# Seven block products on 320 and 256 columns in place of 384 and 192, and a re-searched order of work

## The chip, the cores and the metric

The kernel runs on one core of one Trainium2 chip. Its time is device microseconds from one execution of the whole program; a figure for a kernel is the median of several executions. The core's engines work side by side, each through its own instructions in order, and wait for one another through semaphores: PE (TensorE, the matrix products), DVE (VectorE), ACT (ScalarE), POOL (GpSimd) and SP (SyncE, which only issues transfers here). PE writes to PSUM, eight banks of 512 float32 columns; all else lies in SBUF.

## The reference, cut to what matters

```
a      = softmax of phi over 32 memory slots, per head and token
k_m, v_m = a.T @ k, a.T @ v                     # 32 x 64 per head
attn   = softmax(q @ k_m.T / 8) @ v_m           # 4 x 576 tokens, 8 heads of 64
x      = attn, as 2304 tokens x 512
h      = x @ w_in;  x = (h * sigmoid(1.702 h)) @ w_out          # d_ff 2048
xn     = x / sqrt(mean(x * x) + 1e-6) * rms_g
g      = xn @ w_gate;  val = xn @ w_val                         # d_ff 1536
out    = (g * sigmoid(g) * val) @ w_out2                        # 2304 x 512
```

All in float32. The weights are read as 64-bit numbers and converted on the chip.

## The kernel before, in words

**Tiling.** The four batches of 576 tokens are two pairs of 1152 tokens, `pr` 0 and 1. Activations stand transposed: channels on partitions, tokens along the columns. Float32 products are made of float32r halves: an operand x is held as h (a rounded copy) and l = x - h, and a product is h·h + l·h + h·l. `split` (L745) makes such a pair: a copy on ACT, a subtraction on DVE or POOL. Every matmul has weights of 128x128 that are loaded for it alone, so the instructions on PE are LDWEIGHTS, MATMUL, LDWEIGHTS, MATMUL and so on.

**Stages.** First the attention of the first pair, with the loading and converting of weights; then the first MLP in steps `a_g1` and `a_g2` for `pr` 0 (8 groups of 256 hidden channels), beside it the attention of the second pair; the same for `pr` 1, beside it the norm of the first pair (`norm_1` to `norm_4`); then the second MLP of the first pair (`b_g3`, `b_g4`, 6 groups), beside it the norm of the second pair and the block sums `t_a` to `t_d`; last the second MLP of the second pair, `s_g3` and `s_g4`.

**The last stage.** The second pair's gate and value products are done as a two-by-two block product with seven products in place of eight. The blocks of the activations are 256 channels by 576 tokens (`tba` to `tbd`), those of the weights 256 channels by 128 outputs, and there are 12 groups `f`. `product(q, a, b, f)` (L1321) makes one block product on one of two column ranges `q`, `WIDE[q]` (L1318), columns 0 to 384 and 384 to 576: 6 matmuls into one PSUM bank (two halves of the channels by three terms). Here a product on the first range is called wide, on the second narrow. `s_g3(f, k)` (L1335) calls it for both ranges of all seven: for `k` 0 three block products, for 1 two, for 2 two. Their results are added up on DVE by `plus` (L1332) in four sums `part[q]`; two get a Silu on ACT; each is multiplied with its partner, and the two products of 576 columns, end to end 1152 tokens, are split into three tiles of 384 tokens. The list `to` (L1370) says which columns of which range go to which tile: five splits for each `f`. `s_g4(g, kk)` (L1382) multiplies 128 tokens of two `f` with the output weights, 6 matmuls of 512 columns, and adds into `oacc` on DVE; after the last group `put` writes them out.

**The order.** Nothing of this is issued where it is called. Each operation goes into a list (`Plan.add`, L268), and `Plan.order` (L438) then plays the list through on a model of the engines, with the durations of `Plan.cost` (L307), the buffers of each pool and PSUM, and a due time for each step (`dues`, L397). The operation that can start first goes first, among near ones that with the earliest due time. What comes out is one fixed order for each engine. For a float32r matmul of n columns the model has 0.0135 + n/2400 us (L316). Where PE has nothing to do in the model for long, `fill` (L521) puts in matmuls of 512 columns on constants. Two tables bend this: `HASTE` (L127) makes a named step's due time earlier by so many us, and `OTHER` (L171) moves the named operations of a step (counted from 0 within the step) from POOL to DVE or from DVE to POOL.

Of the kernel before, what the change touches and what calls it, by code (L numbers as in the profile page):

```python
# [10 lines left out]
F32 = mybir.dt.float32  # L11
# [20 lines left out]
class Fill:  # L32
    eng, name = "PE", "matmul"
# [83 lines left out]
class Plan:  # L117
# [18 lines left out]
        "a_g2 0 4 0": 38.2,  # L136
        "a_g2 0 6 0": 22.8,
        "a_g2 0 7 0": 33.4,
        "a_g2 1 1 0": 38.0,
        "a_g2 1 6 2": 45.6,  # L140
        "a_g2 1 7 2": 18.7,
        "att_k3 2 1": 46.5,
# [6 lines left out]
        "att_q3s 0 0 1": 69.7,  # L149
        "att_q4 1 1 0": 86.2,  # L150
        "att_q4 3 0 1": 21.3,
        "b_g4 0 2": 6.4,
        "ld_unit 2 1": 51.8,
        "norm_1 0 1": 60.9,
        "norm_1 1 0": 22.4,
        "norm_2 0 2": 20.2,
        "norm_3 0 1": 66.6,
        "norm_4 0 0 0": 9.7,
        "norm_4 0 0 1": -36.4,
        "s_g3 0 2": 27.8,  # L160
        "s_g4 5 1": 73.1,
        "s_g4 5 5": 13.4,
        "s_g4 5 7": 18.7,
        "s_g4 5 8": 62.3,
        "vm_part 0 3 0": 31.7,
        "vm_part 0 7 0": 56.5,
        "w_conv a 0 2 in 0": 50.3,
        "w_load a 0 7 in 0": 87.4,
    }

    OTHER = {  # L171
        "a_g1 0 0 0": (17,),
        "a_g1 0 0 1": (17,),
        "a_g1 0 1 0": (8, 17),
        "a_g1 0 1 2": (8,),
        "a_g1 0 2 2": (8, 10),
# [13 lines left out]
        "a_g1 0 6 2": (8, 19),  # L190
        "a_g1 0 6 3": (17,),
        "a_g1 0 7 0": (17,),
        "a_g1 0 7 1": (8, 10, 19),
        "a_g1 1 2 0": (17,),
        "a_g1 1 2 1": (21,),
        "a_g1 1 2 2": (8,),
        "a_g1 1 3 0": (8, 17),
        "a_g1 1 4 2": (10, 21),
        "a_g1 1 5 2": (21,),
        "att_k3 1 0": (2,),  # L200
        "att_k3 2 1": (2,),
        "att_q3s 0 0 1": (3,),
        "att_q3s 0 1 0": (3,),
        "att_q3s 1 0 0": (3,),
        "att_q3s 2 0 0": (3,),
        "att_q3s 2 1 1": (3,),
        "att_q3s 3 0 0": (3,),
        "att_q3s 3 0 1": (3,),
        "norm_1 0 0": (3,),
        "norm_1 0 1": (3,),  # L210
        "norm_1 0 2": (2, 5),
        "norm_4 0 0 2": (2,),
        "norm_4 0 0 3": (2,),
        "s_g3 11 2": (39,),
        "t_b 0 0": (1,),
        "w_conv a 0 0 in 1": (1,),
        "w_conv a 0 1 in 1": (1, 7),
        "w_conv a 0 1 out 0": (7,),
        "w_conv a 0 1 out 1": (1, 7),
        "w_conv a 0 2 in 0": (1,),  # L220
        "w_conv a 0 2 out 0": (1,),
        "w_conv a 0 3 in 0": (7,),
        "w_conv a 0 3 in 1": (7,),
        "w_conv a 0 3 out 0": (1,),
# [11 lines left out]
        "w_conv a 0 7 out 1": (1,),  # L236
        "w_conv a 1 0 in 0": (1,),
        "w_conv a 1 0 in 1": (1,),
        "w_conv a 1 0 out 0": (1,),
        "w_conv a 1 1 out 1": (1,),  # L240
        "w_conv a 1 5 in 0": (1,),
        "w_conv a 1 5 in 1": (1,),
        "w_conv a 1 6 in 0": (1,),
        "w_conv a 1 6 in 1": (1,),
        "w_conv a 1 6 out 0": (1,),
        "w_conv a 1 6 out 1": (1,),
    }

    def __init__(self, nc):
# [56 lines left out]
    @staticmethod  # L306
    def cost(op):  # L307
        def size(x):
            return reduce(int.__mul__, (n for s, n in x.ap[1:]), 1)

        n = size(op.out)
        if op.eng == "PE":
            if op.name == "transpose":
                return 0.0009 * n, 0.0009 * n + 0.16
            if op.kw["lhsT"].dtype == F32R:
                t = 0.0135 + n / 2400  # L316
                return t, t + 0.16
            t = 0.094 if size(op.kw["lhsT"]) == 32 else 0.17 if n > 1 else 0.22
            return t, t + 0.25
        if op.eng == "ACT":  # L320
            t = 0.08 + n / 1200
            if op.ins[0].space == bass.MemoryType.PSUM:
                t += 0.13 if op.kw.get("func") is AF.Gelu_apprx_sigmoid else 0.07
            return t, max(t + 0.04, 0.18 + n / 1200)
        if op.eng == "POOL":
            two = op.name == "tensor_tensor"
            each = 0.00215 if two else 0.00104 if op.kw.get("op0") is ALU.mult else 0.00355
            if op.kw.get("op") is ALU.mult:
                each = 0.0016
            t = 0.05 + each * n + (0.1 if two else 0.0)  # L330
            return t, t + 0.05
        if op.eng == "DVE":
            rate = 1920 if Plan.fast(op) else 960
            if op.name == "tensor_reduce":
                n, rate = size(op.ins[0]), 960 if op.ins[0].ap[-1][0] == 1 else 560
            t = 0.075 + n / rate + (0.04 if n < 20 else 0.0)
            if any(x.space == bass.MemoryType.PSUM for x in op.ins):
                t += 0.04
            return t, t + 0.08
        return 0.47, 0.0  # L340
# [213 lines left out]
def kernel(  # L554
# [24 lines left out]
    nc = tc.nc  # L579
    B, H, S, D = q.shape  # L580
    M = phi.shape[3]
# [4 lines left out]
    P = 128  # L586
# [8 lines left out]
    TB = 384  # L595
# [9 lines left out]
    def pool(name, bufs, space=bass.MemoryType.SB, **kw):  # L605
        return Slots(plan, ctx.enter_context(tc.tile_pool(name=name, bufs=bufs, space=space)), bufs, **kw)
# [3 lines left out]
    cvp = pool("cv", 6, spare=3)  # L610
# [22 lines left out]
    def psum(name):  # L633
        return psp.tile([P, 512], F32, tag="ps", name=name)
# [110 lines left out]
    def split(x, h, l, eng=V):  # L745
        A.copy(out=h, in_=x)
        sub_lo(eng, l, x, h)
# [567 lines left out]

    WIDE = (slice(0, TB), slice(TB, S))  # L1318
    part = {}

    def product(q, a, b, f):  # L1321
        ps, n = psum("ps_" + a), WIDE[q]
        ps = ps[:, : n.stop - n.start]
        a, b = wt["s", f][a], tb[b]
        i = 0
        for y, z in ((0, 0), (1, 0), (0, 1)):
            for e in range(2):
                PE.matmul(ps, lhsT=a[y][:, e], rhs=b[:, z, e, n], start=(i == 0), stop=(i == 5))
                i += 1
        return ps  # L1330

    def plus(q, to, x, y):  # L1332
        V.tensor_tensor(out=part[q][to], in0=part[q][x], in1=y, op=ALU.add)

    def s_g3(f, k):  # L1335
        if k == 0:
            part[0] = [cvp.tile([P, 512], F32, tag="cv", name="c")[:, :TB] for i in range(4)]
            c = [vlp.tile([P, 512], F32, tag="vl" + x, name="c") for x in "hl"]
            part[1] = [x[:, o : o + S - TB] for x in c for o in (0, S - TB)]
            for q in range(2):  # L1340
                A.copy(out=part[q][0], in_=product(q, "A11", "B11", f))
            for q in range(2):
                plus(q, 1, 0, product(q, "S2", "T2", f))
            for q in range(2):
                plus(q, 0, 0, product(q, "A12", "B21", f))
        elif k == 1:
            for q in range(2):
                plus(q, 2, 1, product(q, "S3", "T3", f))
            for q in range(2):
                part[q].append(product(q, "S1", "T1", f))  # L1350
                plus(q, 1, 1, part[q][4])
        else:
            for q in range(2):
                plus(q, 3, 2, product(q, "A22", "T4", f))
                A.activation(out=part[q][3], in_=part[q][3], func=AF.Silu)
                plus(q, 2, 2, part[q][4])
                A.activation(out=part[q][2], in_=part[q][2], func=AF.Silu)
            for q in range(2):
                plus(q, 1, 1, product(q, "S4", "B22", f))
            if f % 3 < 2:  # L1360
                ts = [gpp.tile([P, 2, TB], F32R, tag="gp", name="pp") for i in range(NTB)]
            else:
                x = tb["tbd"][:, 1].rearrange("p y e n -> p (y e n)")
                ts = [
                    x[:, 2 * TB * i : 2 * TB * (i + 1)].rearrange("p (y n) -> p y n", y=2)
                    for i in range(NTB)
                ]
            pt["s", f] = ts
            H = TB // 2
            to = [  # L1370
                [(0, 0, 0, TB)], [(1, 0, 0, H)],
                [(1, H, 0, H), (2, 0, H, TB)], [(2, H, 0, H)],
            ]
            for q in range(2):
                for j, (x, y) in enumerate(((0, 3), (1, 2))):
                    o = part[q][x]
                    V.tensor_tensor(out=o, in0=o, in1=part[q][y], op=ALU.mult)
                    for i, d, c0, c1 in to[2 * j + q]:
                        d = slice(d, d + c1 - c0)
                        split(o[:, c0:c1], ts[i][:, 0, d], ts[i][:, 1, d])  # L1380
# [112 lines left out]
    for j, (*key, t) in enumerate(slots):  # L1493
        i = groups.index(tuple(key))
# [39 lines left out]
    for j, (*key, t) in enumerate(slots):  # L1534
        key = tuple(key)
        i = groups.index(key)
# [93 lines left out]
```

## Time and profile before

| | |
|---|---|
| median of 3 runs | 869.61 us (869.45 to 871.04) |
| the profiled execution | 867.26 us, its span 865.5 us |
| granted TensorE clock, mean of the span | 1.000 |
| busy: PE, PEld (weight loads) | 853.2 us (99%), 813.3 us (94%) |
| busy: DVE, ACT, POOL | 668.8 us (77%), 459.3 us (53%), 285.3 us (33%) |

The span is the time from the first to the last instruction of the profiled execution. A busy time is the time covered by an engine's instructions. Successive matmuls overlap in the records, so the duration of one is longer than the time by which it delays the next; the distance between starts is what it takes of PE.

### The profile page before, as it was taken

The numbers are of one execution on the slowest core, as the hardware profiler recorded it, in microseconds if no ns is written. First come the engines' busy times: TensorE is split into PE (matmuls) and PEld (weight loads), VectorE is DVE, ScalarE is ACT, GpSimd is POOL, SyncE is SP. The second block draws the span as 40 slices with busy tenths as digits, with TensorE's granted clock in tenths as the row PEclk, the third lists the DMA queues.
The fourth block names the chain that finished last, engine by engine and source line by source line (L and its number), as shares of the span: only waits on it lengthen the run. The fifth ranks groups of instructions, "written<-read, shape, count | busy, mean of one in ns | idle before, by whom it ended". The sixth has DMA issues, their size and how long they took to land.

```text
span 865.5 us, 15423 instructions
## 1 busy us (share of the span) xinstructions
PE 853.2 (99%) x5644; PEld 813.3 (94%) x5644; DVE 668.8 (77%) x1409; ACT 459.3 (53%) x1073; POOL 285.3 (33%) x308
## 2 busy tenths in 40 slices
PE   8899999999999999999999999999999999999998
PEld 6799999999999999999999999999999999999996
DVE  3979899999962774577786778586679878989875
ACT  3587777767668654564555645333244543433320
POOL 2354565363488675555443233221000000000000
PEclk9999999999999999999999999999999999999999
DMA  9975549734612111242462525331132111202003
GB/s 244 273 209 145 172 122 276 216 83 132 155 51 61 37 49 50 62 146 68 152 218 75 169 99 171 110 121 51 36 104 82 48 38 38 62 13 62 13 1 109
DMA packets 60508, 93.54 MB, mean 108 GB/s; under 512 B 5392, under 2 KB 29968, under 8 KB 60432
## 3 DMA queue, kind: packets, MB, share of 16 engines
q1 hardware_dynamic: 60432, 92.56, 37.0%
q8 instruction: 44, 0.72, 0.4%
q14 instruction: 32, 0.26, 0.1%
HBM read 69.99 MB, written 22.54 MB: 107 GB/s over the span
## 4 chain that ended last, share of the span: by engine, by line
PE 89%; DVE 5%; issue 2%; DMA 2%; ACT 1%; SPq 1%; POOL 0%; DVEq 0%; ACTq 0%; POOLq 0%
PE pg L550 66%; PE ps_S L550 10%; PE ps_A L550 7%; PE pvm L550 2%; PE pq L550 2%; DMA raw_a_out<-in_moe_w_out_dram 2%; DVE pad L550 1%; DVE stage L550 1%; PE pk L550 1%; DVE x L550 1%; SPq L550 1%; DVE kmisc L550 0%; PE pnm L550 0%; ACT pad L550 0%; ACT vm_6h L550 0%
## 5 line engine op out<-in xcount | busy, mean ns | idle before, releaser
L550 PE MATMUL pg<-gr,a_outh 128*128 128x384 f32 (+1 forms) x736 | 196.6, 334 | 0.5 <-POOL gr L550 0.5
L550 PEld LDWEIGHTS pg<-gr,a_outh 128*128 128x128 f32 x736 | 132.9, 188 | 1.6 <-POOL gr L550 1.0
L550 DVE TENSOR_TENSOR x<-x,pg 128x384 f32<-128x384 f32 (+1 forms) x172 | 90.4, 539 | 46.2 <-PE pg L550 44.9
L550 PE MATMUL pg<-gr,a_outl 128*128 128x384 f32 (+1 forms) x368 | 122.0, 331 | 0.0
L550 POOL TENSOR_TENSOR gr<-gf,gr 128x288 fp32r<-128x288 f32 (+2 forms) x135 | 86.5, 660 | 75.2 <-ACT gr L550 49.8
L550 POOL TENSOR_TENSOR tbd<-c,tbd 128x192 fp32r<-128x192 f32 x1 | 0.6, 604 | 250.9 <-ACT tbd L550 250.9
L550 DVE TENSOR_TENSOR oacc<-oacc,pg 128x512 f32<-128x512 f32 x90 | 61.6, 685 | 25.1 <-PE pg L550 23.9
L550 PE MATMUL pg<-b_o2h,pp 128*128 128x512 f32 x216 | 70.7, 393 | 0.0
L550 ACT ACTIVATE gf<-pg 128x288 f32<-128x288 f32 x128 | 51.1, 411 | 35.4 <-PE pg L550 30.2
L550 PEld LDWEIGHTS pg<-gr,a_outl 128*128 128x128 f32 x368 | 69.1, 188 | 0.0
L550 ACT CAST gr<-gf 128x288 fp32r<-128x288 f32 (+2 forms) x184 | 59.3, 360 | 9.8 <-PE pg L550 5.4
L550 DVE TENSOR_TENSOR c<-c,ps_S 128x384 f32<-128x384 f32 (+1 forms) x120 | 53.5, 452 | 14.0 <-PE ps_S L550 10.8
L550 PE MATMUL pg<-s_o,pp 128*128 128x512 f32 x216 | 57.0, 393 | 0.0
L550 DVE TENSOR_TENSOR pf<-sg,pg 128x384 f32<-128x384 f32 x36 | 19.9, 552 | 37.5 <-PE pg L550 25.3
L550 PEld LDWEIGHTS pg<-b_o2h,pp 128*128 128x128 f32 x216 | 40.6, 188 | 8.0
L550 PE MATMUL ps_S<-tbc,s_S 128*128 128x192 f32 (+1 forms) x288 | 47.3, 305 | 0.0
L550 PE MATMUL ps_S<-tbb,s_S 128*128 128x192 f32 (+1 forms) x288 | 47.1, 305 | 0.0
L550 PE MATMUL ps_A<-tba,s_A 128*128 128x192 f32 (+1 forms) x288 | 46.9, 305 | 0.0
L550 PEld LDWEIGHTS pg<-s_o,pp 128*128 128x128 f32 x216 | 39.7, 188 | 7.5
L550 PEld LDWEIGHTS ps_S<-tbc,s_S 128*128 128x128 f32 x288 | 43.9, 190 | 1.1
L550 PEld LDWEIGHTS ps_A<-tba,s_A 128*128 128x128 f32 x288 | 43.4, 190 | 0.7
L550 PEld LDWEIGHTS ps_S<-tbb,s_S 128*128 128x128 f32 x288 | 43.2, 190 | 0.6
(248 smaller groups left out, 2156.8 us busy)
## 6 DMA issues: line engine op xcount, KB each, us to landing
cache<-cv SPq DMA_DIRECT2D x36, 256.0 KB, 2.8
raw_a_in<-in_moe_w_in_dram SPq DMA_DIRECT2D x16, 512.0 KB, 5.3
raw_a_out<-in_moe_w_out_dram SPq DMA_DIRECT2D x16, 512.0 KB, 4.2
cache<-pad SPq DMA_DIRECT2D x32, 256.0 KB, 5.1
raw_b_gate<-in_moe_w_gate_dram SPq DMA_DIRECT2D x12, 512.0 KB, 4.6
raw_b_val<-in_moe_w_val_dram SPq DMA_DIRECT2D x12, 512.0 KB, 4.5
raw_b_o<-in_moe_w_out_dram SPq DMA_DIRECT2D x12, 512.0 KB, 4.1
raw_s_vg<-cache SPq DMA_DIRECT2D x48, 128.0 KB, 2.7
```

The source lines that it names most:

```text
L550: getattr(self.real[op.eng], op.name)(*op.args, **op.kw)
```

## The change

The two column ranges of a block product become 0 to 320 and 320 to 576. The four sums of each range get these widths, and the list `to` is written anew, as the tile borders at 384 and 768 now fall elsewhere: six splits for each `f`, one of them of 64 columns. The planner's duration of a float32r matmul gets a lower bound of 0.109 us. In `HASTE` 11 entries are gone, in `OTHER` entries for 27 operations; no entry is added. As most of these steps name POOL in the code and `OTHER` had them on DVE, 22 operations go from DVE to POOL: nine `sub_lo` of `a_g1` (four of 288 columns, two of 192, three of 96), eight of `w_conv` for `pr` 1 (512 columns), two additions of 384 columns and one of 768 in `norm_1` and its `sub_lo` of 384, and one multiplication in `att_q3s`. Five go from POOL to DVE: one `tensor_scalar` in `w_conv a 0 2 out 0`, two `sub_lo` in `norm_4`, one subtraction in `t_b`, one `sub_lo` in `s_g3 11 2`.

```diff
 HASTE
-        "a_g2 1 1 0": 38.0,
-        "b_g4 0 2": 6.4,
-        "norm_1 0 1": 60.9,
-        "norm_1 1 0": 22.4,
-        "norm_3 0 1": 66.6,
-        "norm_4 0 0 0": 9.7,
-        "norm_4 0 0 1": -36.4,
-        "s_g3 0 2": 27.8,
-        "s_g4 5 1": 73.1,
-        "s_g4 5 7": 18.7,
-        "w_conv a 0 2 in 0": 50.3,
 OTHER
-        "a_g1 0 0 1": (17,),
-        "a_g1 0 7 1": (8, 10, 19),
-        "a_g1 1 2 0": (17,),
-        "a_g1 1 2 1": (21,),
-        "a_g1 1 2 2": (8,),
-        "a_g1 1 3 0": (8, 17),
-        "a_g1 1 4 2": (10, 21),
-        "a_g1 1 5 2": (21,),
+        "a_g1 0 7 1": (10, 19),
+        "a_g1 1 4 2": (21,),
-        "att_q3s 1 0 0": (3,),
-        "norm_1 0 0": (3,),
-        "norm_1 0 1": (3,),
-        "norm_1 0 2": (2, 5),
-        "norm_4 0 0 2": (2,),
-        "norm_4 0 0 3": (2,),
-        "s_g3 11 2": (39,),
-        "t_b 0 0": (1,),
-        "w_conv a 0 2 out 0": (1,),
-        "w_conv a 1 0 out 0": (1,),
-        "w_conv a 1 1 out 1": (1,),
-        "w_conv a 1 5 in 0": (1,),
-        "w_conv a 1 5 in 1": (1,),
-        "w_conv a 1 6 in 0": (1,),
-        "w_conv a 1 6 in 1": (1,),
-        "w_conv a 1 6 out 0": (1,),
-        "w_conv a 1 6 out 1": (1,),
 cost
-                t = 0.0135 + n / 2400
+                t = max(0.0135 + n / 2400, 0.109)
...
-    WIDE = (slice(0, TB), slice(TB, S))
+    WIDE = (slice(0, 320), slice(320, S))
...
-            part[0] = [cvp.tile([P, 512], F32, tag="cv", name="c")[:, :TB] for i in range(4)]
+            part[0] = [cvp.tile([P, 512], F32, tag="cv", name="c")[:, :320] for i in range(4)]
             c = [vlp.tile([P, 512], F32, tag="vl" + x, name="c") for x in "hl"]
-            part[1] = [x[:, o : o + S - TB] for x in c for o in (0, S - TB)]
+            part[1] = [x[:, o : o + 256] for x in c for o in (0, 256)]
...
-            H = TB // 2
             to = [
-                [(0, 0, 0, TB)], [(1, 0, 0, H)],
-                [(1, H, 0, H), (2, 0, H, TB)], [(2, H, 0, H)],
+                [(0, 0, 0, 320)], [(0, 320, 0, 64), (1, 0, 64, 256)],
+                [(1, 192, 0, 192), (2, 0, 192, 320)], [(2, 128, 0, 256)],
             ]
```

## Rows read from the trace of the kernel before

**Rows 1.** Windows over the whole span; columns named in the first line.
```profile
core 0: us, PE busy (x) PEld busy (x) DVE busy (x) ACT busy (x) POOL busy (x), PEclk, DMA share, GB/s
0.00:60.00 60.00, 53.77 (x519) 45.52 (x520) 39.94 (x112) 33.51 (x86) 21.69 (x27) 1.00 0.96 255
60.00:240.00 180.00, 178.15 (x1435) 174.06 (x1434) 171.60 (x366) 135.53 (x339) 94.34 (x92) 1.00 0.56 159
240.00:637.70 397.70, 397.70 (x2344) 384.94 (x2343) 270.37 (x509) 208.55 (x456) 168.69 (x190) 1.00 0.31 96
637.70:861.30 223.60, 223.56 (x1352) 208.79 (x1351) 186.19 (x424) 81.75 (x196) 0.60 (x1) 1.00 0.17 49
```

**Rows 2.** Chain that ended last, in order of time: start us, us, what.
```profile
252.11 3.21 PE pg L550 x24
298.23 1.43 PE pvm L550 x12
641.57 0.65 PE ps_A L550 x6
642.22 1.40 PE pg L550 x6
643.62 1.07 PE ps_A L550 x6
644.69 1.04 PE ps_S L550 x6
645.73 2.76 PE pg L550 x12
650.60 1.32 PE ps_S L550 x12
654.30 1.72 PE ps_A L550 x12
```

**Rows 3.** Groups by form, PE then DVE and ACT, 637.7 to 861.3 us.
```profile
L550 PE MATMUL ps_A<-tba,s_A 128*128 128x192 f32 x144 | 19.5, 271 | 0.0
...
L550 DVE TENSOR_TENSOR pp<-c,pp 128x192 fp32r<-128x192 f32 x32 | 10.4, 352 | 1.0 <-ACT pp L550 0.9
L550 DVE TENSOR_TENSOR pp<-c,pp 128x384 fp32r<-128x384 f32 x8 | 4.4, 552 | 0.1
...
L550 ACT CAST pp<-c 128x192 fp32r<-128x192 f32 x32 | 10.0, 352 | 13.9 <-DVE c L550 13.8
L550 ACT CAST pp<-c 128x384 fp32r<-128x384 f32 x8 | 4.1, 509 | 1.0 <-DVE c L550 0.7
```

**Rows 4.** Timeline of DVE near the end: start us, us, instruction [idle before].
```profile
854.28 0.36 DVE L550 TENSOR_TENSOR tbd<-c,tbd 128x192 fp32r<-128x192 f32 x1 [0.47 <-ACT tbd L550]
861.30 0.69 DVE L550 TENSOR_TENSOR oacc<-oacc,pg 128x512 f32<-128x512 f32 x1 [0.67 <-PE pg L550]
```

**Rows 5.** Groups by form on POOL, whole span.
```profile
L550 POOL TENSOR_TENSOR gr<-gf,gr 128x288 fp32r<-128x288 f32 x51 | 43.8, 866 | 44.5 <-ACT gr L550 29.7 <-PE pg L550 11.3 <-issue 3.2
L550 POOL TENSOR_SCALAR pad<-pad 128x512 f32<-128x512 f32 x14 | 29.9, 2138 | 15.2 <-ACT pad L550 15.2
L550 POOL TENSOR_TENSOR a_outl<-raw_a_out,a_outh 128x512 fp32r<-128x512 f32 x12 | 15.8, 1317 | 2.1 <-DVE sr L550 1.5
L550 POOL TENSOR_TENSOR sq<-sq,sq 128x768 f32<-128x768 f32 x5 | 9.5, 1904 | 18.7 <-ACT sq L550 10.8 <-PE pg L550 7.9
```

**Rows 6.** Windows of 20 us where POOL is fullest; columns as in rows 1.
```profile
240.00:260.00 20.00, 20.00 (x145) 19.97 (x144) 11.99 (x27) 14.53 (x33) 16.50 (x21) 1.00 0.21 60
260.00:280.00 20.00, 20.00 (x135) 19.95 (x134) 4.88 (x9) 15.85 (x42) 15.97 (x21) 1.00 0.21 58
```

**Rows 7.** Groups by form on PE, whole span: the constant matmuls.
```profile
L550 PE MATMUL pk<-ones_r 128*128 128x512 f32 x37 | 11.8, 462 | 1.3 <-DVE ones_r L1410 1.3
L550 PE MATMUL pk4s<-ones_r 128*128 128x512 f32 x22 | 5.5, 392 | 0.0
L550 PE MATMUL pq<-ones_r 128*128 128x512 f32 x11 | 2.9, 396 | 0.0
```

## The prediction

> **What bounds the kernel now.** I read the page first: PE is busy 99% of the span at full clock, every other engine 77% or less. Busy time alone does not say that PE sets the end, so I cut the span into stages [rows 1]. From 240 to 861.3 us PE is covered without a gap to speak of (397.70 of 397.70 us, then 223.56 of 223.60); before 240 us it is open for 6.2 us and then 1.9 us, and holds 70 matmuls on constants of 11.8 + 5.5 + 2.9 = 20.2 us, which the planner put in where it expected PE to wait [rows 7]. So two things set the end: what the products take on PE from 240 us on, and some 28 us of waiting in the first 240 us. The last stage, 637.7 to 861.3 us, is where the column ranges are used, and there DVE is busy 186.19 us of 223.60 and ACT 81.75. Then I read the chain of waits in order of time, for it gives what a product really takes: from its first matmul to the first of the next [rows 2].
>
> **A narrow product costs more than its columns.** Six matmuls of 384 columns take 1.04 us (173 ns each); twelve of 256 take 1.43 us (119 each); 24 of 288 take 3.21 us (134 each). Between 256, 288 and 384 that is 0.41 to 0.46 ns a column, and carried on to 192 columns it would give 92 ns. But six matmuls of 192 take 0.65 us, 108 ns each, and twelve in a row 1.32 us [rows 2]. Below 256 columns something else sets the pace; weights are loaded for every matmul, and the weight loads cover 208.79 us of this stage's 223.60 [rows 1], so I take it to be the loading. It shows once more behind a narrow product: a wide product that follows one takes 1.07 us in place of 1.04, an output unit of 512 columns 1.40 in place of 2.76 / 2 = 1.38 [rows 2].
>
> The Trainium skill ("TensorE: Matmul & The Clock Gate", Back-to-back issue gap) speaks against the change. It gives a warm gap of N/2.4 + 2.5 ns for a matmul alone, and about 81 ns at 128 columns and 131 at 512 for a stream with weight loads. Either is straight in the columns, and 384 + 192 would then cost what 320 + 256 costs. Here the rows disagree: from 192 to 256 columns the matmul gains 11 ns, from 256 to 384 it gains 54. The same page has 128 columns of weights at P/1.2, 107 ns, close to the 108 measured.
>
> **Part 1, the new widths.** 12 groups with 7 block products each are 84 pairs of a wide and a narrow product, 6 matmuls a product; the row for two of the seven products has 144 narrow matmuls [rows 3]. The pair before: 1.04 + 0.65 = 1.69 us where nothing pays behind it, 1.07 + 0.65 = 1.72 where the next product does, which is what a row of twelve shows, and the commonest row of this stage. After: 320 columns do not occur, and lie a third of the way from 288 to 384, 134 + (173 - 134)/3 = 147 ns, so 0.88 us; 256 columns 0.715 us; together 1.60. The saving is 0.09 to 0.12 us a pair, 84 times that 7.8 to 10.3 us. I take 9.5, nearer to the upper end, as most narrow products are followed by a wider one. All of it is PE time in a stretch without a gap, so it is on the path as long as nothing else becomes late.
>
> **What it adds there.** The sums keep their number and together their 576 columns, so DVE's additions and multiplications cost the same. One split more for each of 12 groups, of 64 columns: on DVE 352 ns at 192 columns and 552 at 384 give 1.04 ns a column, so 0.22 us, 2.6 us in all; on ACT 352 and 509 give 0.25 us, 3.0 in all [rows 3]. The cover is the matmuls: DVE has 186.19 + 2.6 = 188.8 us to do in 223.6 - 9.5 = 214.1 us (88%), ACT 84.8 us (40%). I cost it at nothing; without cover it is 2.6 us. One tile's data now come from both ranges: tile 0 needs 64 columns of the second. Those are of the sum that is ready before the last block product, so nothing waits for the last one that did not before. The PSUM banks and the buffers stay in number and size.
>
> **The end.** The last narrow product becomes 256 columns wide. Addition, multiplication, copy and subtraction behind it grow by 64 columns each, some 0.25 us by the slopes above. The last such subtraction ends at 854.64 us; the last two output units, 1.38 us each, start no sooner than about 858.5, as the last addition starts at 861.30 [rows 4]. 3.9 us of cover: nothing. What follows the last matmul (0.69 us of DVE and the transfer out) stays.
>
> **Part 2, the lower bound in the planner.** 0.0135 + n/2400 passes 0.109 at 229 columns, so it touches only the 192 columns that go and the 128 of `norm_2`. A pair of the old widths counted 0.1735 + 0.0935 = 0.267 us for a matmul of each, one of the new 0.1468 + 0.1202 = 0.267: the old plan already assumed a PE as fast as the new one is, and kept DVE and ACT up with it on paper. That is why I expect no new wait in the last stage.
>
> **Part 3, the tables.** 22 operations go to POOL. From its rows [rows 5], taking the nearest wider form where there is no own row: nine `sub_lo` of `a_g1` at up to 0.87 us (7.8), eight of `w_conv` at 1.32 (10.5), one addition of 1.90, four of 384 columns at up to 1.32 (5.3): up to 25.5 us more for POOL. Five go back to DVE. Of the 22, 18 fall into the stretch from 240 to 637.7 us, where POOL is busy 168.69 of 397.70 us and PE never waits; there they cost nothing as long as POOL stays ahead, though at 240 to 280 us it is busy 32.47 of 40 [rows 6]. Four fall before 240 us (288 and 96 columns of `a_g1`, one of `w_conv` at 1.32, the multiplication), at most 4.4 us for POOL; there DVE is the full one (171.60 of 180), and gets lighter by them, and POOL is rid of a conversion of 2.14 us [rows 5]. So the bounds are a gain of some 2.1 us, should that conversion have been on the path, and a loss of 4.4, should all four be. I take 0, nearer to the gain. The eleven due times move steps within waits that the same bounds hold; three of them are in the last stage, which has no wait to give.
>
> **Sum.** 867.26 - 9.5 + 0 + 0 = 857.8 us in the terms of the profiled execution (span 865.5 and 1.76 us around it). The median of the runs lies 2.35 us above that execution, so the forecast is 857.8 + 2.35 = 860.1, say 860.2 us. Its own range is from 869.61 - 10.3 - 2.1 = 857.2 to 869.61 - 7.8 = 861.8.
>
> **The rivals.**
> 1. The first 240 us get longer. The order there is a chain of hand-overs at 95% DVE, and any change of order can open a gap. For: 28 us of waiting are there to grow. Against: DVE loses work. All four operations exposed: 860.2 + 4.4 = 864.6.
> 2. DVE becomes the bound at places of the last stage. For: 88% on average leaves little where it is bunched. Against: 25 us are left over, and the old plan allowed for this pace. With the 12 added subtractions all on the path, 860.2 + 2.6 = 862.8.
> 3. Slower: POOL becomes the bound between 240 and 380 us. It has 81% at 240 to 280 us and gets the `a_g1` and `w_conv` operations there; a late `sub_lo` holds the `a_g2` product that reads it, and PE issues in order. From 9.5 of the 25.5 us exposed, that is 37%, the gain is gone; at half it is 869.61 - 9.5 + 12.8 = 872.9. Against: POOL would still be under 90% in the fullest stretch (one `w_conv` and one or two `a_g1` operations come to its 32.47 us), an `a_g2` step comes a whole step after its `a_g1`, and the planner plays POOL's time through.
> 4. The change does nothing: matmul time is straight in the columns, all four widths at one rate. The 84 pairs then save nothing, 869.6. The rows for 192 and 256 columns speak against it; only a pace that the matmuls of 256 columns lose among the others of this stage could bring it about. (The Trainium skill's gap, above, is this case.)
>
> **Chances.** Forecast 0.73; rival 1 0.11; rival 2 0.08; rival 3 0.05; rival 4 0.03. The range: 857.0 to 864.5, from the forecast's lower end to almost all of rival 1. A measurement of this kernel tells 0.2% (1.7 us) from no change. Faster: the forecast and rivals 1 and 2, 0.92. Same: rival 4 and the few cases of rival 3 near its turning point, 0.04. Slower: 0.04.
>
> **What would show it.** In the chain of waits of the changed kernel a pair of block products takes 1.60 us, six matmuls of 320 columns 0.88 and of 256 0.72, with nothing extra behind a 256. The stage from the first block product to the last matmul is about 214 us in place of 223.6, with PE covered throughout; the start of that stage stays at 637.7 within 3 us. POOL's busy time grows by some 15 to 20 us, without a wait of PE for POOL. The prediction is wrong if six matmuls of 256 columns take more than 0.75 us, if PE waits for DVE in the last stage, or if the last stage begins later by more than 4 us.

## The result and the profile after

| | before | changed kernel | ratio (95% interval) |
|---|---|---|---|
| first comparison | 870.33 us | 858.88 us (858.35 to 862.01, 4 runs) | 0.9875 [0.9848, 0.9903] |
| again, beside the experiments (e10) | 867.55 us | 860.27 us (858.03 to 863.04, 6 runs) | 0.9904 [0.9874, 0.9935] |

The forecast was 860.2 us, in a range from 857.0 to 864.5. By the two ratios the kernel became 11 and 8 us faster; their intervals together allow 6 to 13.

The stages of the changed kernel, the first three cut at the times of [rows 1], the last at its own; columns as there:

```profile
0.00:60.00 60.00, 52.60 (x498) 43.95 (x499) 39.50 (x110) 31.79 (x81) 21.78 (x27) 1.00 0.96 249
60.00:240.00 180.00, 178.03 (x1427) 172.44 (x1427) 169.20 (x357) 135.42 (x338) 91.73 (x90) 1.00 0.56 159
240.00:637.70 397.70, 397.32 (x2350) 384.32 (x2349) 263.06 (x493) 208.68 (x453) 185.45 (x210) 1.00 0.31 95
...
642.00:856.00 214.00, 213.63 (x1355) 198.99 (x1353) 185.22 (x439) 83.87 (x209) 0.00 (x0) 1.00 0.18 51
```

PE is still covered to the end, which now comes at 856 us in place of 861.3. DVE is busy 185.22 of the last 214.0 us, 87%, where 88% was worked out. POOL's busy time between 240 and 637.7 us rose from 168.69 to 185.45 us.

The chain of waits, in the stretches that answer to [rows 2] (start us, us, what):

```profile
656.72 1.60 PE ps_S L516 x12
658.32 1.60 PE ps_A L516 x12
...
748.34 0.72 PE ps_A L516 x6
749.06 1.39 PE pg L516 x6
750.45 0.88 PE ps_A L516 x6
...
844.72 10.92 PE pg L516 x48
```

A pair takes 1.60 us where it took 1.72; six matmuls of 256 columns 0.72, of 320 columns 0.88, and the output unit behind a 256 takes 1.39, as it does elsewhere. From the start of the first block product's first matmul to that of the kernel's last matmul it is 212.37 us, where it was 222.91: 10.5 us less.

The span of this profiled execution is only 5.3 us shorter, for that stage began at 642.9 us, 4.9 later than in the profile of before. That execution was the slowest of the four. What of the 4.9 us is the change and what the execution is the second question for the experiments; e7 to e10 answer it.

### The profile page after: what moved, and what is told of

Its sections match the earlier page's. It is cut to its first block, busy times and chain, and to the rows that moved or that the text cites. A ratio compares the mean times of both kernels' runs of the same rounds, so it can differ in the third digit from the quotient of the medians.

```text
span 860.2 us, 15412 instructions
## 1 busy us (share of the span) xinstructions
PE 845.9 (98%) x5645; PEld 803.4 (93%) x5645; DVE 661.0 (77%) x1404; ACT 463.5 (54%) x1087; POOL 299.0 (35%) x325
## 4 chain that ended last, share of the span: by engine, by line
PE 88%; DVE 6%; DMA 2%; ACT 1%; issue 1%; SPq 1%; POOL 0%; ACTq 0%; POOLq 0%
PE pg L516 65%; PE ps_S L516 9%; PE ps_A L516 7%; PE pvm L516 3%; DMA raw_a_out<-in_moe_w_out_dram 2%; PE pq L516 2%; DVE pad L516 1%; DVE stage L516 1%; PE pk L516 1%; DVE x L516 1%; SPq L516 1%; DVE kmisc L516 1%; DVE gr L516 1%; DMA cache<-pad 0%; PE pnm L516 0%
## 5 line engine op out<-in xcount | busy, mean ns | idle before, releaser
L516 POOL TENSOR_TENSOR gr<-gf,gr 128x192 fp32r<-128x192 f32 (+2 forms) x144 | 93.2, 669 | 64.6 <-ACT gr L516 48.0
L516 DVE TENSOR_TENSOR c<-c,ps_S 128x320 f32<-128x320 f32 (+1 forms) x120 | 52.8, 450 | 9.8 <-PE ps_S L516 8.0
L516 PE MATMUL ps_S<-tbb,s_S 128*128 128x320 f32 (+1 forms) x288 | 44.2, 296 | 0.0
L516 PE MATMUL ps_A<-tba,s_A 128*128 128x320 f32 (+1 forms) x288 | 43.7, 296 | 0.0
L516 PE MATMUL ps_S<-tbc,s_S 128*128 128x320 f32 (+1 forms) x288 | 43.7, 296 | 0.0
L516 PE MATMUL pg<-b_o2l,pp 128*128 128x512 f32 x108 | 42.3, 392 | 0.0
L516 ACT ACTIVATE sg<-pg 128x384 f32<-128x384 f32 x36 | 17.7, 491 | 45.6 <-PE pg L516 35.2
L516 PEld LDWEIGHTS ps_S<-tbc,s_S 128*128 128x128 f32 x288 | 40.9, 190 | 0.8
```

The source lines that it names most:

```text
L516: getattr(self.real[op.eng], op.name)(*op.args, **op.kw)
```

## The experiments

"Widths alone" is the kernel before with the new column ranges and list of splits; tables and planner costs stay. Each ratio is to the kernel before, timed beside it on the same chip.

**e1, the widths alone.** The edit is the last three hunks of the diff (`WIDE`, `part`, `to`).

> The kernel before with the new widths alone: ranges of 320 and 256 columns, the sums and the list of splits, but the old tables and the old durations in the planner. The order is that of before up to the last stage. Theory A (the weight load sets about 108 ns a matmul below 256 columns, and the whole gain is the pairs): 84 pairs at 1.60 us in place of 1.715, 9.7 us less, ratio 0.988 to 0.989; last stage about 213.5 to 214 us, the rest unchanged. Rival B (much of the gain is the re-searched order before 637 us): about half, ratio 0.994. Rival C (matmul time straight in the columns): ratio 1.000.

857.03 us, ratio 0.9864 [0.984, 0.9889]. In the chain of waits:

```profile
654.83 1.60 PE ps_S L550 x12
656.43 1.60 PE ps_A L550 x12
```

The last stage takes 212.35 us and starts at 637.8. On every engine the order up to it is that of before, so the widths by themselves give the whole gain. Rivals B and C fall.

**e2, the tables and the lower bound alone.** The changed kernel, with

```diff
-    WIDE = (slice(0, 320), slice(320, S))
+    WIDE = (slice(0, TB), slice(TB, S))
...
(part and to likewise as before)
```

> The changed kernel with the old widths of 384 and 192 back: new tables and the lower bound of 0.109 us in the planner alone. Theory A: within 0.2% of before (ratio 0.998 to 1.001), the last stage again about 223.6 us. Rival B: ratio 0.994. Rival D (the tables cost time that the widths paid for, POOL late between 240 and 380 us): above 1.002, with waits of PE for POOL there.

870.49 against 868.88 us, ratio 1.0013 [0.9996, 1.003]: no gain, so rival B falls once more; a cost of 0.1 to 0.3% can neither be told from nothing nor excluded, and rival D stays open here. The last stage is back at 222.88 us, and a pair at 1.72:

```profile
657.81 1.72 PE ps_A L516 x12
```

**e5, lighter weights.** The kernel before, with this in `product`:

```diff
-                PE.matmul(ps, lhsT=a[y][:, e], rhs=b[:, z, e, n], start=(i == 0), stop=(i == 5))
+                m = P if q == 0 or i in (0, 5) else 96
+                PE.matmul(
+                    ps[:m], lhsT=a[y][:, e, :m], rhs=b[:, z, e, n], start=(i == 0), stop=(i == 5)
+                )
```

> The kernel before; in each narrow product the middle four of six matmuls load only 96 of the 128 weight columns and give 96 output rows, so a part of the sum is left out for rows 96 to 127. Columns streamed, order and number of instructions stay. Theory A, that the load is the pace: these four go from 108 ns to the pace of their 192 columns, 92 to 94 ns, or to 96/128 of 108 = 81 if that is higher, so 84 x 4 x 15 ns = 5.0 us less, and up to 1 us more behind them: ratio 0.993 to 0.9945. Rival E (a fixed time for each matmul, whatever it loads): 108 ns still, ratio 1.000.

861.88 us, ratio 0.9912 [0.9889, 0.9935]; the last stage 215.55 us, 7.4 less than before. The chain shows a narrow product behind a wide one, then one pair:

```profile
644.56 0.56 PE ps_A L550 x6
...
655.23 1.63 PE ps_S L550 x12
```

192 columns are streamed as before, yet six matmuls take 0.56 us in place of 0.65. By the starts of the matmuls the five distances inside such a product are 87 to 91 ns, and from its sixth, with full weights behind it, to the next product it is 113; in the kernel before the first distance is 88, the others 109 to 116. So the pace of a narrow product goes with the 128 weight columns, as it would if loading them sets it; rival E, a fixed time a matmul, falls. Fewer weight columns are also fewer output rows, and e5 does not part the two: that it is the load is the simpler reading, not shown by itself. The gain was larger than expected, since 192 columns alone go below the 92 ns to which I had carried on the rows of 256 to 384.

**e4 and e3, other widths.** The changed kernel with 448 and 128, and with 352 and 224 columns; for e4:

```diff
-    WIDE = (slice(0, 320), slice(320, S))
+    WIDE = (slice(0, 448), slice(448, S))
...
-                [(0, 0, 0, 320)], [(0, 320, 0, 64), (1, 0, 64, 256)],
-                [(1, 192, 0, 192), (2, 0, 192, 320)], [(2, 128, 0, 256)],
+                [(0, 0, 0, 384), (1, 0, 384, 448)], [(1, 64, 0, 128)],
+                [(1, 192, 0, 192), (2, 0, 192, 448)], [(2, 256, 0, 128)],
```

> The changed kernel with 448 and 128 columns. Theory A: narrow products keep 108 ns a matmul, so 0.65 us though they have a third fewer columns than 192; wide ones 200 ns, 1.20 us, and 0.03 behind a narrow one; a pair 1.87 us in place of 1.715, 84 x 0.155 = 13 us more than before, ratio 1.014 to 1.016. Rival C: the same columns, so the time of the changed kernel or of before, ratio 0.988 to 1.000.

885.92 us, ratio 1.0212 [1.017, 1.0253]. Last stage 237.95 us, 15.0 more than before; the widths are the only difference from e2. In the chain a wide product, two narrow ones and a pair:

```profile
654.29 1.24 PE ps_A L516 x6
655.53 0.62 PE ps_S L516 x6
656.15 0.67 PE ps_A L516 x6
656.82 1.91 PE ps_S L516 x12
```

> The changed kernel with 352 and 224 columns, just below the width at which columns and load cross. Theory A: 160 ns a matmul for the wide, and about 110 for the narrow (the load, where 224 columns alone would take 106): a pair 1.62 us against 1.598, the last stage 1.5 to 2.5 us longer than 212.4. Rival J (below 256 columns the time goes on falling with the columns down to some 200): 212.4 us.

863.27 us, ratio 0.9931 [0.9901, 0.996]; last stage 215.19 us, 2.8 more than with 320 and 256:

```profile
653.31 0.96 PE ps_A L516 x6
654.27 0.66 PE ps_S L516 x6
654.93 0.67 PE ps_A L516 x6
655.60 1.63 PE ps_S L516 x12
```

Where a narrow product follows another, six matmuls of 128, 192 and 224 columns take 0.67, 0.66 (half of 1.32 in [rows 2]) and 0.67 us; of 256 columns 0.72. The floor is flat below, and the crossing lies between 224 and 256 columns. So rival J falls (e3), and C (e4). e4 came out 2.0 us dearer than expected and e3 0.3 us above its range: a narrow product's shortfall is also paid by the product behind it (the first matmul of 448 columns behind a 128 takes 255 ns, the others 206), and 206 ns is itself above the 200 that had been put down for 448 columns.

**e6, three times the short subtractions.**

```diff
                         split(o[:, c0:c1], ts[i][:, 0, d], ts[i][:, 1, d])
+                        if c1 - c0 < 192:
+                            for again in range(2):
+                                sub_lo(V, ts[i][:, 1, d], o[:, c0:c1], ts[i][:, 0, d])
```

> The changed kernel with more work for DVE in the last stage: the two shortest splits of each group (64 and 128 columns) do their subtraction three times, with the same result: 48 subtractions more, 24 of about 0.22 us and 24 of about 0.29, 12.2 us by their records, over four times the 2.6 us that the change added. Theory A (DVE has room beside PE): last stage 212.4 us within 1 us and no wait of PE in it. Rival I (DVE is about to be the bound there): last stage longer by 4 us or more, PE waits for DVE.

861.1 us, ratio 0.9906 [0.9879, 0.9932]. The last stage:

```profile
642.00:856.00 214.00, 214.00 (x1357) 199.40 (x1355) 194.01 (x488) 84.01 (x211) 0.00 (x0) 1.00 0.19 52
```

DVE is busy 194.01 us of 214, where the changed kernel has 185.22, and PE waits for nothing: 212.37 us from first to last matmul, as without them. At 91% busy DVE still holds nothing up; rival I falls.

**e7 to e10, where the tables' part lies.** e7 is e1 once more, e8 is e1 with the new `OTHER`, e9 is e1 with the new `HASTE`, e10 the changed kernel.

> The kernel before with the new widths alone once more, as the mark for the other three of this series. Theory A: again 0.986 to 0.989 of before; last stage 212.4 us; its start 637.7 to 641.2 us, as far as two executions of the old order lay apart already.

> New widths, old due times, new engine table (22 operations back on POOL, 5 on DVE). Theory F (the engine table costs some 1 to 2 us, since subtractions on DVE meet long additions on POOL and wait, as at 245 us in the changed kernel): 0.001 to 0.002 above the widths alone, PE waits between 210 and 390 us. Rival G (the tables do nothing that can be told): equal within 0.1%.

> New widths, old engine table, new due times (11 entries gone). Theory F: equal to the widths alone within 0.1%. Rival H (it is the due times that cost the 1 to 2 us): 0.001 to 0.002 above the widths alone, and the waits there. Rival G: equal.

> The changed kernel as it is, beside the widths alone on the same chip. Theories F and H: 1 to 2 us above the widths alone. Rival G: equal within 0.1%. Last stage 212.4 us in either.

| | us | ratio to before | last stage, start and length |
|---|---|---|---|
| e7, widths alone | 858.78 | 0.9885 [0.9859, 0.991] | 640.0, 212.35 |
| e8, with `OTHER` | 857.83 | 0.9874 [0.985, 0.9898] | 639.4, 212.35 |
| e9, with `HASTE` | 857.66 | 0.9872 [0.9848, 0.9897] | 637.0, 212.37 |
| e10, all | 860.27 | 0.9904 [0.9874, 0.9935] | 641.7, 212.37 |

By the times neither table alone costs anything, so F and H are not borne out; the whole is 1.5 us slower than the widths alone, within the intervals. The profiles say more. With both new tables and the bound (the first profile, e2, e4, e10, e6 and e3) the last stage starts at 641.2 to 643.4 us, with the old tables and costs (before, e1, e7, e5) at 637.8 to 641.1. And all six of the first kind have a wait near 245 us that none of the other seven has. In the first profile, DVE, POOL and PE in turn (timeline: start us, us, instruction):

```profile
244.74 0.56 DVE L516 TENSOR_REDUCE stage<-pq 96x12 f32<-96x384 f32 x1 [0.81 <-issue]
245.33 1.79 DVE L516 TENSOR_TENSOR gr<-gf,gr 128x192 fp32r<-128x192 f32 x1
```
```profile
245.07 1.83 POOL L516 TENSOR_TENSOR sq<-sq,sq 128x768 f32<-128x768 f32 x1
```
```profile
246.55 0.33 PE L516 MATMUL pg<-gr,a_outl 128*128 128x384 f32 x1
247.26 0.59 PE L516 MATMUL pg<-gr,a_outh 128*128 128x384 f32 x2 [0.38 <-DVE gr L516]
```

A subtraction of 192 columns, 0.35 us elsewhere [rows 3], takes 1.79: it starts 0.26 us behind POOL's addition of `norm_1` and ends 0.22 us behind it, and the matmul that reads it comes 0.71 us behind the one before, in place of 0.17. A second such meeting, of two `a_g1` subtractions with a `w_conv` one near 235 us, makes PE wait for `kz` by 0.3 to 1.3 us in the same six. Together that is 0.8 to 1.8 us, which fits the 1.0 to 1.6 us by which the ratios set e2 above before (1.0013), the changed kernel above e1 (0.9875 to 0.9864) and e10 above e7 (0.9904 to 0.9885). That the waits come with the two tables together is shown; by the intervals above, that the whole times differ is not.

The way to the last stage can be timed by itself. From the first matmul of the attention output (the 372nd, at 46 to 49 us) to the first block product PE has the same matmuls in every profile, save one more of 512 columns on constants in the new order. A meeting of DVE and POOL at 217 us, told of at the end, falls in some executions and not in others, so like goes beside like:

| first attention output to last stage | with the meeting | without it |
|---|---|---|
| both tables and the bound | 594.1 to 595.6 us (first profile, e2, e3, e4, e6) | 592.8 us (e10) |
| none of them, or one | 593.2 to 593.8 us (e5, e7, e11) | 591.0 to 592.1 us (before, e1, e8, e9) |

By these averages the new order is 1.3 to 1.4 us slower on this way. That sorts the 4.9 us of the first profile. 2.1 lie before the first attention output, no more than executions of the new order differ there (45.9 to 48.9 us). 1.7 are the meeting, which e10 does without. 0.8 are the two waits above, and so the change's. What the last 0.3 are stays open.

The end differs too. Behind the last matmul's start come 4.96 to 4.99 us in the seven profiles with the new due times (e9 among them) and 4.40 to 4.41 in the four with the new widths and the old ones (4.61 before). The last addition on DVE, in the first profile and in e1:

```profile
855.66 0.69 DVE L516 TENSOR_TENSOR oacc<-oacc,pg 128x512 f32<-128x512 f32 x1 [0.67 <-PE pg L516]
```
```profile
850.53 0.69 DVE L550 TENSOR_TENSOR oacc<-oacc,pg 128x512 f32<-128x512 f32 x1 [0.67 <-PE pg L550]
```

From its end to that of the span, 860.2 and 854.5 us, the transfers out take 3.85 and 3.3 us. So the new due times cost 0.6 us there; which of the eleven does it was not tried.

**e11, the lower bound with the widths.**

```diff
-                t = 0.0135 + n / 2400
+                t = max(0.0135 + n / 2400, 0.109)
```

> New widths and the lower bound of 0.109 us in the planner, old tables. The order differs from that of the widths alone in a few places around the norm's products. Theory A: last stage 212.4 us, ratio as for the widths alone, 0.986 to 0.9885; the bound by itself does nothing.

858.61 us, ratio 0.9881 [0.9843, 0.9919], last stage 212.35 us from 639.0. As expected; the bound itself does nothing that can be told.

## Why the prediction was right, and where it was off

**Part 1, the widths.** Right in mechanism and close in size. The forecast saving of 9.5 us was 10.5 in every profile: all eight with 320 and 256 columns have 212.35 to 212.37 us, the two with 384 and 192 and full weights 222.9. By the starts of all matmuls, six wide ones take 1.065 us on average and six narrow 0.651, together 1.716; now 0.881 and 0.717, together 1.598. 84 times 0.118 is 9.9 us. The rest lies in what I had counted only for wide products: an output unit behind a narrow product pays too, 253 ns for its first matmul in place of 229, in 20 places, 0.5 us. The term "most narrow products are followed by a wider one" was thus undersized; the upper bound of 10.3 us was nearer, and still 0.2 short.

**What it adds there.** Right: 64 columns cost DVE 0.22 us (the rows of after have 1.7 us for 8 of them, 218 ns each), and the cover holds with 48 subtractions more (e6).

**The end.** Right for the last narrow product: no matmul waits for what hangs on it. The stretch behind the last matmul keeps its form, 0.69 us of DVE and the transfer, but is 0.35 us longer than before; the widths alone make it 0.2 shorter, the due times 0.6 longer.

**Part 2.** Right as far as tried: no wait of PE in the last stage, and e11 (0.9881) is where e7 is (0.9885).

**Part 3, the tables, at 0.** This is the weak step. Its bounds (a gain of 2.1, a loss of 4.4) hold, but the value was taken at the wrong end: the new order has at least two waits that the old has not, and takes 1.3 to 1.4 us longer to the last stage. They did not come the way of rival 3, by POOL being full (its busy time there grew by 16.8 us, as foretold): a subtraction on DVE waited out an addition on POOL. Nor did the due times cost nothing: three of them are in the last stage, and with the new ones the end is 0.6 us longer, though PE waits for nothing. My sign for it, a last stage that begins over 4 us later, was met in the first profile (4.9 us) and in e6 (5.4), not in e10 (3.7); with starts that differ by 3.4 us between executions of one order it was too sharp for a single profile.

**The sum.** 860.2 against 858.88 and 860.27 us. Two errors nearly cancel: the widths gave 1 us more, the tables by the profiles took 1 to 2. That the number is so close is luck in part: the 2.35 us by which the median was set above the profiled execution are no property of a kernel, for in the changed kernel that execution lies 3.1 us above the median.

**The gap that was weighed.** Six matmuls of 128, 192, 224 and 256 columns take 0.67, 0.66, 0.67 and 0.72 us, so a gap straight in the columns, as the prediction read the figures of the Trainium skill ("TensorE: Matmul & The Clock Gate", Back-to-back issue gap), does not hold for this stream of loads and matmuls. The same page's time for a weight load (LDWEIGHTS (loading the stationary operand)), P/1.2 = 107 ns at 128 columns, agrees with 0.65 / 6 = 108 ns, and e5 with its being the load.

Of the versions run, the widths with the old tables (e1, e7), or with one of the new ones (e8, e9), come out at 857.0 to 858.8 us, at or below the changed kernel each time; the differences lie within the intervals.

## What to carry to other kernels

Where each matmul brings its own weights, look in the trace for the width below which the distance between starts stops falling (here between 224 and 256 columns), and split an uneven range so that no part lies below it: the number of columns and of matmuls stays, and here the time fell by 10.5 us. Read such a cost from the starts, together with what the next product pays, not from a matmul's own duration. A schedule searched on a model of the engines can be worth nothing on the chip, as here: test it by itself, and look for waits that every execution of it has. Where the whole time scatters too much, time a stretch in which all versions do the same work.

## What the hardware showed beyond that

**DVE waits out an addition on POOL, and a race decides.** Besides the subtraction above, a `TENSOR_SCALAR` of 12 elements on DVE does it, in the changed kernel's profile (first DVE, then POOL, then PE):

```profile
217.18 1.95 DVE L516 TENSOR_SCALAR stage<-stage 96x12 f32<-96x12 f32 x2
```
```profile
217.27 1.83 POOL L516 TENSOR_TENSOR kmisc<-kmisc 96x768 f32<-96x768 f32 x1 [2.86 <-ACT kmisc L516]
```
```profile
218.85 0.42 PE L516 MATMUL pg<-attnT,vm_7h 128*128 128x288 f32 x2
219.95 0.50 PE L516 MATMUL pg<-attnT,vm_7h 128*128 128x288 f32 x2 [0.67 <-DVE stage L516]
```

In the profile of before the same two operations took 0.28 us, for there both were begun before POOL's addition. Here the addition starts 0.09 us behind the first of them and the second waits for its end; the matmul of PE that hangs on it starts 0.96 us behind the one before. This meeting, and some 0.7 us more of waiting behind it, is in 8 profiles (old and new tables alike: the first of the changed kernel, e2, e3, e4, e5, e6, e7, e11) and not in 5 (before, e1, e8, e9, e10). In the 8 the addition starts 0.02 to 0.04 us ahead of the second operation, in 4 of the 5 it starts with it or up to 0.05 us behind. Laid beside before, which has the same order, e7 falls back by 1.7 us between 216 and 224 us and makes up none of it on the way to the last stage. So it is one reason why equal orders end 2 to 3 us apart; the rest of that spread, up to 2.9 us of it before 30 us, was not followed up. The Trainium skill ("SBUF — State Buffer", Who interferes with whom) says that a DVE instruction with two SBUF inputs contends with a GpSimd instruction that reads SBUF, that one in a 2-port mode contends with GpSimd, and that whoever issues first has the ports which the two share for its whole instruction. The durations here agree: 1.79 us beside 1.83. Which mode the `TENSOR_SCALAR` ran in no run here shows.
